# Row-tiled attention scores from the sixth pair of heads on instead of the seventh, with a new table of due dates

## The chip, the cores and the metric

The kernel runs on one core of a Trainium2 chip, as one program in which TensorE (PE), VectorE (DVE), ScalarE (ACT), GpSimd (POOL) and SyncE (SP) work side by side. The metric is the device time of one execution in microseconds. The kernel before took 307.12 us, the median of five runs (306.81 to 309.54).

## The reference

Two layers follow each other. The first is block-sparse attention over 4 batches, 8 heads, 768 tokens and 64 features a head. The mask goes by blocks of 32 tokens: neighbours, the first and last block, and three drawn blocks a query block.

```python
scores = scale * np.matmul(q, k.transpose(0, 1, 3, 2))
mask = np.abs(blk_i - blk_j) <= window
mask = mask | (blk_i == 0) | (blk_j == 0) | (blk_i == n_blocks - 1) | (blk_j == n_blocks - 1)
...                                     # and the sampled blocks of each query block
attn = softmax(np.where(mask, scores, -1e9))
return np.matmul(attn, v)
```

The heads are put side by side (768 x 512 a batch) and go through a residual MLP:

```python
a1 = alpha1 * x + beta1
u = x + lam * np.einsum('ts,bsd->btd', w_tok, a1)       # mixes tokens
a2 = alpha2 * u + beta2
return u + lam * (np.maximum(a2 @ w_ch1, 0.0) @ w_ch2)  # 512 -> 2048 -> 512
```

## The kernel before

**Pairs and units.** The 32 (batch, head) combinations are taken as 16 pairs of heads, four pairs a batch. Scores are computed transposed, keys on partitions, and each pair's 2 x 768 x 768 scores are cut into 9 units of 128 x 1024. A unit goes through four steps: its scores on TensorE into PSUM; the exponential on ScalarE into an SBUF tile `eT` (seven of them), line 1057; in the row form a multiplication with the mask on VectorE, line 1062; and the product with the values on TensorE, line 1081, which also gives the sums for the division (lines 1097 and 1100).

**Two forms of scores**, told apart by `T0`. Pairs below `T0` use the *full* form. Their q and k are transposed by TensorE (line 517, twelve transposes a pair), four copies bring them from PSUM to SBUF (lines 576 on ScalarE, 578 on VectorE), and a matmul contracts over 88 rows: 64 features and 24 rows that hold the mask as a bias (line 1019). One unit is one operation of the planner. Pairs from `T0` on use the *row-tiled* form (`prep_rows`). Their q and k are transposed by DMA on SP's queue, three transfers a pair (lines 915 and 938); the two halves of each query buffer are also needed on the other 64 partitions, which two moves do (line 959; DMAs for pairs 6 and up, VectorE copies for a pair below 6). The contraction has 64 rows, and two matmuls run at once in the upper and lower half of the array (line 1038). One operation of the planner is a batch of three units; two of the units lie in two-bank PSUM tiles (`sps`), the third in two single banks (`gb`), whose exponential is done in two halves. The mask of the row form is computed once, by 12 small matmuls from the buffers of pair `T0 - 1` (line 806), an exponential (line 820) and ten copies into `msk` (line 832 and one after it).

**The other stages.** After a batch's pairs are normalised, x is scaled and shifted (lines 1253 and 1264), tokens are mixed (`tok`, line 1302, with w_tok transposed on TensorE at the start), u is formed (lines 1326 and 1340), and the two channel matmuls follow (`ch1`, line 1449, its ReLU at line 1488 on ScalarE or 1496 on VectorE; `ch2`, line 1529, and the last sum at line 1551). The scaling vectors `lam`, `a1` (alpha1), `b1` (beta1) and `a2` (alpha2) are loaded as broadcasts; token mixing needs the first three.

**What sets the order.** A planner (`Plan`) writes the program. Each operation has a list of engines that can run it with a cost, dependencies, the buffers it needs, and a due date in units (about 1 us apart). `Plan.run` steps through modelled time and gives each idle engine, among the operations that are ready and find their buffers free, the one with the smallest due date; the instructions are emitted in that order, and the order is fixed on each engine. Loads run in one modelled queue (`queued`), SP's transfers beside them (`beside`). A pair's transposed q and k have two buffers in all (`qk`), and raw q, k and v four each. A due date is a base from a formula plus a hundredth of an entry of the table `DUE`, entry by entry in the order in which the operations were added:

```python
for op, x in zip(pl.ops, DUE):
    op.due += x * 0.01
pl.run()
```

The first entries are those of wtk 0 to 2 (bases -4, 1, 2), the broadcasts lam, a1, b1, a2 (8, 8.1, 8.2, 16), four parts of w1 (24 to 27), then k, q and v of each pair. The base of the loads of q and k is `9 * pi - 12` for pairs below `T0` and `9 * pi - 20` from it on.

Of the kernel before, what the change touches and what calls it, by code (L numbers as in the profile page):

```python
# [45 lines left out]
T0 = 6  # L46
FINE = 3
DUE = [
    -3320, -4973, -4124, -2497, -3795, -94, -4291, 3313, 2359, 2331, -861, -5555, -5734, -3452, -4351, -4448,
    -4315, -638, -1806, 2418, 1986, -1493, 1958, 1931, -1716, 1224, 1688, -2528, 53, 1439, -341, 3700, 125,  # L50
    742, -4865, 5401, 2785, 4715, -531, -4901, -2475, 3984, 913, -3830, 5751, 9883, -2111, -215, 10152, -5717,
    1842, -7686, 748, -1316, 16146, 1379, -1773, -1993, -1719, -178, -17140, 2893, -11188, -12305, -3457, 182,
    -6674, -6907, -2346, -10621, -794, 3980, -5076, -203, 2648, -1691, -2758, -3166, -3178, 11068, -2537,
    -3434, 7487, -1999, -10741, -4678, -7266, -870, -10374, -996, 0, 0, 0, 0, 0, 0, 0, 0, 0, 0, 0, 0, 0, 0, 0,
    0, 0, 0, 0, 0, 0, 0, 0, 0, -5099, -6292, -10397, -6299, 3643, -7374, -10673, -9328, -6545, -2679, 2050,
    3212, -7799, -10612, -10005, -9083, -4760, -10523, -13207, -5336, -3600, -6148, 5224, -13270, 894, -1963,
    4971, -8368, 19587, 4850, 6731, -2817, 5395, -19447, 2663, 5944, -9167, -10839, -8054, -2150, 5871,
    -11026, -3278, -5093, 5470, -1761, -735, 182, 5882, 2231, 3836, -6607, -963, -84, 3197, -5604, -4701,
    -8847, -4544, 1423, -5386, -3880, -2292, -1085, -2445, 5311, -3851, 4130, -2333, -694, 0, 0, 9060, -11409,
    -3670, -6195, 0, 0, 4307, -1082, -5729, -10780, 0, 0, 3630, -2020, -5854, -6594, -788, 992, 2804, 310,  # L60
    486, -4798, 2399, -1962, 4764, 118, 3925, 7540, -5227, -3529, 6170, -2580, 5023, 757, -3488, -5436, 1160,
    5708, 5926, 3276, -6650, 6353, 8432, 4371, 3728, 6630, -5542, -4044, 4798, 6193, -6752, 5993, 8994, -533,
    1275, -5131, -7973, -10760, 861, -8296, -12995, -6273, -1450, -8559, -6956, -6232, -677, -5807, -6900,
    -10086, 1173, -7413, -3525, 4331, 1542, -5413, -2264, -8282, -15528, -3823, -11284, -344, -6138, -10239,
    -1938, -9077, 2100, -10737, -11446, 5447, 1599, -5555, -9202, -11839, -6291, -6113, -767, -3507, -4951,
    3673, -7548, -4630, 6000, -3463, -3921, 461, 3395, -1614, 3316, -7396, 5447, -2586, 5102, 378, -540,
    -2951, 4594, 880, -406, -1267, 5243, -4379, 8689, 4355, 3064, -3464, -5400, -1231, 8372, 1238, 7813,
    -7145, 5460, -6781, -3993, -5397, 5226, 1459, 1212, -6142, 2371, 6649, -349, -2533, 220, 4405, -34, 5109,
    4523, -5837, 2213, 124, -7774, 6239, -8726, 5220, -1036, -3161, -487, -1056, -13293, 3244, -2643, 2371,
    2592, -1357, 550, 4360, -7264, 18900, -55, -2161, 5474, 3291, 6317, 3135, 3508, -15586, -7698, -6100,  # L70
    -7503, 1137, -3258, -6008, -4078, -1346, -6586, -817, -3836, 6211, 2410, 1955, -7224, -6685, -7259, 136,
    3165, -4495, -2968, 3328, -2401, 1738, -12609, -3332, -4744, -8040, 3294, -3495, -779, -4106, 3848, 173,
    -4068, 449, 3057, 1513, 5312, 2185, 2201, -2589, -1691, -2575, 5539, 1031, 10211, -2421, -923, 614, 3643,
    -704, -2117, -826, -2410, -2501, -497, -957, 4071, 683, 966, 1081, -26, -2558, 2545, -5958, -5659, -5275,
    -3076, -3121, -2934, -8288, 596, -265, 8788, -2681, 32, 3687, -3940, 4036, -345, -12468, -5978, -4694,
    -4109, -7828, -3022, -12204, -9197, -1796, -13036, 1017, -8655, -2715, 215, -12248, -1218, 7488, -4328,
    -155, 20, 312, -1077, -4136, 11082, -6529, -5888, -5300, 2783, 9055, -3505, 1177, 5249, 7142, 705, -3825,
    720, -1106, -3238, 992, -5532, 2237, -4603, 1964, -1970, 1009, -11287, -1932, -5980, -2093, -4879, -6892,
    -7820, 4360, -1100, -2993, 1852, -2438, 2137, -981, -7198, -6575, 1694, 1702, 3767, -6928, -7962, 3583,
    -9, -313, 512, 6802, 1457, 7109, -1617, 1680, -3802, -11748, 6822, 9939, -3661, -668, 4217, -365, -4539,  # L80
    -6964, 3855, 8630, -6438, 6555, -5493, 397, 1871, 104, -3907, -3520, -12610, 3890, -2298, -8952, -7709,
    -1034, 696, 3003, -5565, -11962, -6900, -7633, -2777, -2200, -3843, 5861, -5613, -591, -14430, -6326,
    1159, -282, -2272, -10693, -9822, 4015, 7719, -4088, 2380, -11269, -4553, 6242, -286, -4895, 3165, 1836,
    3998, -6333, -4739, 8162, 11837, -4302, 4438, 1835, -4226, -4645, -8200, -1834, 2630, -4607, 2490, -4646,
    9296, 3217, 3014, 8088, -1828, 1218, 4557, 1285, 1332, 557, -1916, 6043, -12, 13666, 4828, -4915, -1346,
    -537, -211, -1810, -3117, 1718, -5470, -6241, -15807, -4699, -3758, 1735, 1320, 44, -3218, -1665, -674,
    -3409, -10059, 10265, 1161, 1003, 2339, -6710, 11942, 5208, -3774, -3373, -287, 4786, 4702, -5032, -661,
    874, 4162, -2466, 1539, -8357, -4375, -6611, -13472, -6697, -1302, 6112, 2597, -5260, -3454, -719, -7674,
    -4425, 1397, -201, 4462, -7237, -4471, 4190, 13085, 7488, 12366, 11408, 6073, -6413, -4366, -5909, -736,
    -801, -5381, 8333, 3871, 1899, -9586, -7333, -1970, 4774, -20, 1963, 5481, 1546, 7302, 3234, 4459, -3025,  # L90
    2524, 116, -5796, 2307, 3971, -857, 1183, 1185, -2394, -526, 9256, -4431, 2692, 8027, -6981, 9387, 979,
    -2400, 6532, 463, -1237, 3375, -2440, -3084, -11031, -3313, -8817, 3237, -12826, -412, 10805, 3442,
    -23829, -5087, 7711, 4847, 5045, -2820, 10599, 4625, 6705, 20731, 4944, 14197, 4144, 8980, 10175, -1121,
    6493, -342, 8838, 4280, 11178, 12600, 71, 6755, 13382, 584, -8512, -7532, -9377, 5505, 4922, 1188, 12796,
    12696, 12651, 21122, -2065, -3302, -4344, 424, -2662, -9160, -7126, -3927, -2624, -8204, -2640, 5219,
    -6189, 1350, -8839, -1613, -307, -3382, -703, 4460, -3373, -6771, -2302, -415, -3014, 5547, 5378, 2103,
    -149, 3588, 9640, 9236, 10329, 3977, 989, -63, 3536, -3956, -793, 823, 6219, -10205, 5510, -5653, -2158,
    -2265, -4052, 2538, -3992, -2730, -5898, 1903, -240, -5846, -5735, -5358, -2361, 1826, 1234, -246, 967,
    -141, -6788, 2256, 3669, -332, -5309, -4898, -6464, -523, 125, 2070, 993, -4256, -8406, 23, -7868, -2579,
    -1517, -3907, -2545, -7444, 4499, 2201, 2305, -4315, -716, -847, 1109, -837, -1865, 823, 620, -74, 3256,  # L100
    62, 618, -3542, -824, 6019, -1828, 1584, 4025, -2170, 4111, -4414, -3854, -4591, -1217, -4567, -2014, 100,
    3587, -2582, 1206, -6364, 636, 1239, 8009, -1897, 1751, 6060, 1080, -9779, 4499, -1225, -7744, -4604,
    -1748, -4068, -11085, -4489, -7447, -1652, 1972, 2416, -7520, -3783, 4563, -731, 573, -163, 1736, -6327,
    2720, 4442, -2964, -2233, -6335, -4681, 447, -3120, 4487, -4525, 1368, -6234, 4316, 571, -655, 5271, 3958,
    -5701, -5374, -5929, -5950, 2436, -5387, -665, -2333, 9969, -12579, -703, 201, 3405, 813, 5509, -863, 375,
    3698, -5396, -8886, 4957, 4553, 358, -3480, -6286, 5126, -119, 4979, 537, -9373, -4074, -3406, -1563,
    4030, 7977, 5202, -10863, 2264, -5107, 4188, -4549, 3252, -6595, -36, -2835, 2186, -3110, -1052, 3721,
    -9708, -6967, -5167, -7406, -11272, 7752, 876, -8691, 619, -7394, -5574, -1069, 3293, -2643, 2523, -7011,
    -975, 5444, -5258, 1155, -2123, -3704, -1937, -2176, -11087, -3670, 2625, 7632, -9034, 58, -510, 2162,
    -2293, -3097, 5274, -3580, -4226, 3684, 9443, -1440, -884, -5931, -4516, -5482, -8502, -2036, -4404,  # L110
# [254 lines left out]
def kernel(  # L365
# [274 lines left out]
    def load_pair(pi, what="qkv"):  # L640
        b, n = divmod(pi, NPAIR)
        for w in what:
# [3 lines left out]
            def emit(op, key=key, src=src, w=w):  # L646
# [4 lines left out]
                1000,  # L651
                9 * pi - (6 if w == "v" else 12 if pi < T0 else 20),
                emit,
# [143 lines left out]
    def mask_ops():  # L797
        key = ("mmr",)
        due = 9 * T0 - 10

# [263 lines left out]
    def emit_pv(op, part, pi, u, a):  # L1064
# [3 lines left out]
        for c in part:  # L1068
# [3 lines left out]
            r = s % 36  # L1072
            if pi < T0:
                jt, t = divmod(r, NT)
# [543 lines left out]
```

## Time and profile before

| | before |
|---|---|
| median of five runs | 307.12 us |
| profiled execution | 307.31 us, span 305.5 us |
| granted clock of TensorE | 1.00 |
| instructions | 7143 |
| busy PE / DVE / ACT / POOL | 297.0 / 234.1 / 177.3 / 44.6 us |
| DMA | 31.38 MB, mean 103 GB/s; over 160 GB/s in nearly all of the first 75 us |

The span runs from the first to the last instruction of the profiled execution. Busy time of PE overstates its work, since a matmul is recorded from its start to its modelled end and the next one starts before that; start-to-start distances in the timeline are the better measure. In the lists of instruction groups, a line gives the source line, engine, operation, tiles, shape and count, then busy time and mean length, then the engine's idle time before them and who ended it.

Landings of the first loads by the trace's semaphore events, in us from the span's start (the order is that of issue):

| k1 | q1 | wtk1 | wtk2 | k2 | q2 | wtk0 | v1 | v2 | a1 | a2 | lam | k3 | b1 | q3 |
|---|---|---|---|---|---|---|---|---|---|---|---|---|---|---|
| 9.32 | 10.48 | 12.28 | 14.13 | 16.47 | 16.83 | 18.61 | 19.65 | 20.61 | 22.07 | 24.10 | 25.20 | 26.19 | 26.82 | 28.09 |

The next ones are k6 28.79, k4 29.75, v8 30.76 and w1 (its last quarter) 33.24. The last part of w1 lands at 48.76, the last of w2 at 63.30.

### The profile page before, as it was taken

How to read it: one execution, taken by the hardware profiler on the slowest of the kernel's cores; microseconds unless marked ns; L12 is line 12 of the kernel's file. 1: busy time of each engine (PE TensorE's matmuls, PEld its weight loads, DVE VectorE, ACT ScalarE, POOL GpSimd, SP SyncE). 2: the span in 40 equal slices, each digit the busy share in tenths (PEclk: the TensorE clock that was granted, in tenths of full speed). 3: DMA queues.
4: the chain of work that ended last, by engine and by line, in shares of the span. 5: the costliest groups of instructions: out<-in, count | busy, mean ns of one | idle time of the engine just before them, and what ended most of it. 6: DMA issues, size and time to landing. Idle time of an engine off the chain costs nothing.

```text
span 305.5 us, 7143 instructions
## 1 busy us (share of the span) xinstructions
PE 297.0 (97%) x2970; PEld 186.4 (61%) x2991; DVE 234.1 (77%) x441; ACT 177.3 (58%) x242; POOL 44.6 (15%) x71
## 2 busy tenths in 40 slices
PE   7897999999999999999999999999999999999996
PEld 3675888766666576466655565555664674565443
DVE  7777889988988995979877896668868682897212
ACT  5897998987788755775477655654657720000000
POOL 9456533140210110020000000000000000000000
PEclk9999999999999999999999999999999999999999
DMA  7999999999895879074171544050020004000111
GB/s 163 190 198 208 204 204 185 179 209 168 123 158 98 138 133 163 7 130 103 28 126 34 115 54 79 35 137 11 36 52 36 34 2 121 36 0 0 71 65 72
DMA packets 50672, 31.38 MB, mean 103 GB/s; under 512 B 27784, under 2 KB 47056, under 8 KB 50640
## 3 DMA queue, kind: packets, MB, share of 16 engines
q0 software_dynamic: 17520, 15.47, 33.4%
q1 hardware_dynamic: 32796, 15.06, 22.8%
q8 instruction: 23, 0.38, 0.5%
q10 hardware_dynamic: 324, 0.39, 0.4%
q14 instruction: 9, 0.07, 0.1%
HBM read 30.78 MB, written 6.29 MB: 121 GB/s over the span
## 4 chain that ended last, share of the span: by engine, by line
PE 88%; DMA 7%; POOL 2%; issue 1%; ACT 1%; DVE 0%; POOLq 0%; ACTq 0%
PE gb L1449 27%; PE gb L1529 27%; PE gb L1302 10%; PE gb L1081 10%; PE sps L1019 5%; PE sps L1038 4%; DMA wtk<-in_moe_w_tok_dram 4%; PE gb L1038 3%; DMA q<-in_q_dram 3%; PE gb L517 1%; POOL k L647 0%; ACT eT L1057 0%; POOL q L647 0%; ACT qk L576 0%; POOL wtokT L469 0%
## 5 line engine op out<-in xcount | busy, mean ns | idle before, releaser
L1057 ACT ACTIVATE eT<-sps 128x1024 f16<-128x1024 f32 x114 | 110.6, 1029 | 11.0 <-PE gb L1081 5.7
L1449 PE MATMUL gb<-uT,w1b 128*128 128x384 bf16 (+1 forms) x512 | 91.8, 326 | 0.0
L1529 PE MATMUL gb<-w2b,hts 128*128 128x512 bf16 (+2 forms) x379 | 87.2, 370 | 1.1
L1449 PEld LDWEIGHTS <-w1b 128*128 128x128 bf16 x512 | 48.5, 98 | 33.7 <-issue 1.9
L1062 DVE TENSOR_TENSOR eT<-eT,msk 128x1024 f16<-128x1024 f16 x90 | 59.6, 683 | 6.4 <-ACT eT L1057 6.4
L1529 PEld LDWEIGHTS <-hts 128*128 128x128 bf16 x400 | 36.6, 98 | 38.9 <-issue 1.9
L1057 ACT ACTIVATE eT<-gb 128x512 f16<-128x512 f32 x60 | 32.5, 594 | 33.8 <-PE gb L1038 31.8
L1496 DVE TENSOR_SCALAR hts<-gb,b1t 128x384 bf16<-128x384 f32 x73 | 44.8, 616 | 9.1 <-PE gb L1449 7.6
L1081 PEld LDWEIGHTS <-eT 128*128 128x128 f16 x1152 | 44.3, 97 | 10.8 <-issue 2.2
L1081 PE MATMUL gb<-vext,eT 128*128 128x65 f16 x1152 | 47.9, 193 | 0.1
L1488 ACT ACTIVATE hts<-gb,b1t 128x384 bf16<-128x384 f32 x55 | 31.5, 582 | 21.3 <-PE gb L1449 19.1
L1302 PE MATMUL gb<-a1p,wtokT 128*128 128x256 bf16 (+1 forms) x360 | 37.0, 251 | 0.0
L1551 DVE TENSOR_TENSOR ot<-x_sb,gb 128x512 f32<-128x512 f32 (+2 forms) x25 | 16.6, 664 | 26.0 <-PE gb L1529 26.0
L1302 PEld LDWEIGHTS <-wtokT 128*128 128x128 bf16 x360 | 29.5, 98 | 6.9 <-issue 1.9
L1019 PE MATMUL sps<-qk 88*128 88x512 bf16 (+1 forms) x144 | 31.3, 325 | 0.6 <-ACT eT L1057 0.3
L1326 DVE TENSOR_TENSOR x_sb<-x_sb,gb 128x512 f32<-128x512 f32 (+1 forms) x26 | 16.7, 641 | 2.8 <-PE gb L1302 2.4
L1100 DVE TENSOR_TENSOR x_sb<-gb,rcp 128x384 f32<-128x384 f32 x32 | 17.8, 557 | 1.1
L1038 PE MATMUL sps<-qk 64*128 64x256 bf16 x180 | 17.9, 305 | 0.0
L1340 DVE TENSOR_TENSOR ub<-x_sb,a_bc 128x512 bf16<-128x512 f32 (+1 forms) x26 | 16.1, 644 | 0.3
L1097 DVE RECIPROCAL rcp<-gb 128x6 f32<-128x6 f32 x32 | 6.1, 192 | 13.3 <-PE gb L1081 13.2
L1038 PEld LDWEIGHTS <-qk 64*128 64x128 bf16 x240 | 9.3, 94 | 11.5 <-issue 7.1
L647 POOL DMA_DIRECT2D v<-in_v_dram x15 | 10.6, 704 | 36.3 <-DVE vext L1119 24.7
(70 smaller groups left out, 171.1 us busy)
## 6 DMA issues: line engine op xcount, KB each, us to landing
out_dram<-ot SPq DMA_DIRECT2D x23, 256.0 KB, 2.1
v<-in_v_dram POOLq DMA_DIRECT2D x16, 192.0 KB, 8.5
k<-in_k_dram POOLq DMA_DIRECT2D x15, 192.0 KB, 7.6
q<-in_q_dram POOLq DMA_DIRECT2D x15, 192.0 KB, 7.6
w1b<-in_moe_w_ch_dram POOLq DMA_DIRECT2D x4, 512.0 KB, 11.3
w2b<-in_moe_w_ch_dram POOLq DMA_DIRECT2D x4, 512.0 KB, 17.4
qk<-qk SPq DMA_DIRECT2D x20, 96.0 KB, 2.5
wtk<-in_moe_w_tok_dram POOLq DMA_DIRECT2D x3, 384.0 KB, 8.4
```

Source lines behind the costliest of these rows:

```text
L1019: nc.tensor.matmul(spsT[sl(key[0])][:, o : o + w], kx2[i][0:KC, a, ts(jt, P)], qx2[i][0:KC, a, c : c + w], start=True, stop=True,)
L1038: nc.tensor.matmul(half(key, r)[:, o : o + w], kd[i][rows, h, g, :], qx2[i][rows, h, c : c + w], start=True, stop=True,)
L1057: nc.scalar.activation(out_, in_, AF.Exp, bias=EXPB, scale=SCALE)
L1062: nc.vector.tensor_tensor(out=e, in0=e, in1=msk[:, :, x : x + 512], op=ALU.mult)
L1081: nc.tensor.matmul(bk[:, t * VW : t * VW + D + 1], eTt[sl(("eT", i))][:, ts(col, P)], vx[:, a, jt, 0 : D + 1], start=(r == 0), stop=(r >= ...
L1100: nc.vector.tensor_tensor(out=x_sb[:, s0 : s0 + NT, h * D : (h + 1) * D], in0=o[:, :, 0:D], in1=rc[:].unsqueeze(2).broadcast_to([P, NT, D] ...
L1302: nc.tensor.matmul(bank(bk)[:, j * wp * P : (j + 1) * wp * P], wtokT[:, s, ts(m * g + j, P)], a1p[sl(ak)][:, s, 0:wp, :].rearrange("p w c ...
L1326: nc.vector.tensor_tensor(out=s, in0=s, in1=tp, op=ALU.add)
L1449: nc.tensor.matmul(bank(bk)[:, 0 : HS + w0], w1b[:, dk, ts(f, P)], rhs[dk], start=(dk == 0), stop=(dk == 3),)
L1488: nc.scalar.activation(htsT[hk][:, f, :], bank(bk)[:, w0 : HS + w0], AF.Relu, bias=b1t[:, f : f + 1], scale=1.0,)
L1496: nc.vector.tensor_scalar(out=htsT[hk][:, f, :], in0=bank(bk)[:, w0 : HS + w0], scalar1=b1t[:, f : f + 1], scalar2=0.0, op0=ALU.add, op1=A ...
L1529: nc.tensor.matmul(bank(ck)[:, cs], htsT[hk][:, nk, ts(mt, P)], w2h["t"][:, nk, cs], start=(nk == 0), stop=(nk == 15),)
```

## The change

`T0` goes from 6 to 5, and every entry of `DUE` is replaced. The planner, its costs and its modelled landing times, the operations and the buffers stay as they are.

```diff
-T0 = 6
+T0 = 5
 FINE = 3
 DUE = [
-    -3320, -4973, -4124, -2497, -3795, -94, -4291, 3313, 2359, 2331, -861, -5555, -5734, -3452, -4351, -4448,
...
+    -3684, 199, -845, -288, -1686, -4441, 2523, 2253, 3785, 2762, -783, -617, -789, 450, 524, 817, 1058, 468,
...
 ]
```

For pair 5, `T0 = 5` takes away four TensorE operations of three transposes each, four PSUM copies and nine one-unit score operations. In their place come two DMA transposes of q and one of k, two half-swaps on VectorE (pair 5 is below 6), nine mask multiplications and three batches of row-tiled scores. Both tables have 1408 entries. The mask is built from pair 4's buffers instead of pair 5's, its base due dates are 9 earlier, and the loads of q and k of pair 5 have the base 25 instead of 33.

## The prediction

> **What bounds the kernel now.** I read the busy shares, then the chain that ended last, then TensorE's own waits. The two lines below, from the page, give busy time and the chain by engine.
>
> ```profile
> PE 297.0 (97%) x2970; PEld 186.4 (61%) x2991; DVE 234.1 (77%) x441; ACT 177.3 (58%) x242; POOL 44.6 (15%) x71
> ...
> PE 88%; DMA 7%; POOL 2%; issue 1%; ACT 1%; DVE 0%; POOLq 0%; ACTq 0%
> ```
>
> Busy PE alone would prove little, since a matmul's recorded length overlaps the next one's. The chain says more: 88% of the span is TensorE after TensorE, and the 7% of DMA lies before 28.1 us. The waits of PE say the same, in us, times, longest:
>
> ```profile
> PE gb L517 <- DMA q<-in_q_dram: 1.7, 1, 1.7
> PE gb L517 <- DVE relp L512: 1.0, 1, 1.0
> PE gb L485 <- PEq L1602: 0.8, 1, 0.8
> PE gb L517 <- ACT relp L541: 0.4, 1, 0.4
> PE gb L485 <- DVE ot L1551: 0.4, 1, 0.4
> PE sps L1019 <- ACT eT L1057: 0.3, 1, 0.3
> ```
>
> All of PE's waits make 4.6 us, and after 30 us there is no single one above 0.3 us but a dummy matmul at the very end. The granted clock is 1.00 in every stretch that the windows below show. So a microsecond of TensorE work that goes away is a microsecond off the end, as long as no other engine or transfer makes PE wait in its place.
>
> **PE work removed and added.** From the timeline of PE I take distances from start to start. The first lines hold pair 5 (the sixth) as it is now, the last ones a batch of three row-tiled units of a later pair (columns: start, length, instruction, count).
>
> ```profile
> 57.17 1.04 PE L1019 MATMUL sps<-qk 88*128 88x512 bf16 x5
> 58.05 0.33 PE L517 MATMUL gb<-identb,q 128*128 128x128 bf16 x3
> 58.22 0.33 PE L517 MATMUL gb<-identb,k 128*128 128x128 bf16 x3
> 58.38 0.82 PE L1449 MATMUL gb<-uT,w1b 128*128 128x385 bf16 x4
> 59.04 0.60 PE L1019 MATMUL sps<-qk 88*128 88x256 bf16 x3
> 59.48 2.13 PE L1449 MATMUL gb<-uT,w1b 128*128 128x385 bf16 x12
> ...
> 87.08 0.54 PE L1081 MATMUL gb<-vext,eT 128*128 128x65 f16 x12
> 87.55 0.39 PE L1038 MATMUL gb<-qk 64*128 64x512 bf16 x2
> 87.78 0.60 PE L1038 MATMUL sps<-qk 64*128 64x256 bf16 x6
> 88.31 0.82 PE L1449 MATMUL gb<-uT,w1b 128*128 128x384 bf16 x4
> ```
>
> Two full units (five matmuls) take 58.05 - 57.17 = 0.88, one takes 59.48 - 59.04 = 0.44 us: nine units 3.94. Three transposes take 0.17 (58.05 to 58.22); pair 5 has twelve: 0.67. Both go. A row-tiled batch takes 88.31 - 87.55 = 0.76 us from its first matmul to the next other one. Before it, 12 matmuls of 65 columns, at 65/128 of a transpose's 0.056 us so 0.028 to 0.03 each, end near 87.46, so entering costs about another 0.09. Three batches: 3 x 0.85 = 2.55. Saved: 3.94 + 0.67 - 2.55 = **2.06 us**. The 12 small matmuls for the mask (L806) only move from pair 5 to pair 4.
>
> *The skill on this.* The Trainium skill, "TensorEngine Tiling (Array Packing)", section Theoretical Speedup, gives up to 2x for a contraction of 64 or less; its section Key Properties says that a change of tiling mode drains the array. By 2x alone the three batches would cost 1.97 and the saving be 2.64; the trace's 2.55, with the 0.09 us at the entry of a batch, is the drain at work, and the trace decides.
>
> **VectorE and ScalarE.** The row form masks after the exponential instead of in the matmul. From the page's groups:
>
> ```profile
> L1057 ACT ACTIVATE eT<-sps 128x1024 f16<-128x1024 f32 x114 | 110.6, 1029 | 11.0 <-PE gb L1081 5.7
> L1062 DVE TENSOR_TENSOR eT<-eT,msk 128x1024 f16<-128x1024 f16 x90 | 59.6, 683 | 6.4 <-ACT eT L1057 6.4
> L1057 ACT ACTIVATE eT<-gb 128x512 f16<-128x512 f32 x60 | 32.5, 594 | 33.8 <-PE gb L1038 31.8
> ```
>
> DVE gains nine mask multiplications, 9 x 0.683 = 6.15. It gains two half-swaps (for this pair on DVE, not by DMA), which the trace lacks: bounded by 0 and by the dearest copy of 768 columns within SBUF, 0.456 (L996); I take the nearest in width and speed, 0.351 (L1119), so 0.7 and at most 0.9. Of the four PSUM copies of pair 5 that go, one ran on DVE (0.56) and three on ACT (3 x 0.789 = 2.37). In each batch one exponential of 1029 ns becomes two of 594: ACT gains 3 x 0.159 = 0.48. Net: DVE +6.3, ACT -1.9 us. The ten mask copies (L832: 9 of 404 to 594 ns, about 4 us in all with the last) move up from 72 to 76 us, ahead of pair 5's first multiplication.
>
> Do these find room? Columns of the windows: stretch, length, busy us of PE, PEld, DVE, ACT, POOL, clock, DMA share, GB/s.
>
> ```profile
> 28.00:57.00 29.00, 28.83 (x474) 24.13 (x474) 26.07 (x53) 26.37 (x29) 12.37 (x18) 1.00 1.27 199
> 57.00:73.00 16.00, 15.90 (x170) 10.64 (x170) 13.68 (x37) 12.82 (x19) 4.91 (x7) 1.00 1.30 194
> 73.00:110.00 37.00, 36.84 (x369) 22.44 (x370) 34.47 (x66) 29.14 (x43) 6.33 (x9) 1.00 0.81 124
> ```
>
> Pair 5's scores lie in 57 to 73. DVE and ACT idle there for 2.3 + 3.2 = 5.5 us; wanted are 6.3 - 1.9 + 4 = 8.4. The excess of 2.9 us must go to neighbours, and ACT alone idles 7.9 us in 73 to 110. ReLUs can run on either engine (616 ns on DVE, 582 on ACT), so about ten of them moving to ACT rebalance it. I cost this at nothing; if the cover fails, 2.9 us shared by two engines hold PE up by about 1.5.
>
> *A rule that speaks against the change.* The same page, section PSUM Bottleneck, warns that tiling speeds up TensorE but not the emptying of PSUM. By the trace that is so: pair 5's exponentials go from 9.26 to 9.74 us while its scores go from 3.94 to 2.55. Were ACT the bound in this stretch, the change would cost 0.5 us instead of gaining 2. PE's waits on ACT after 30 us are 0.3 at most, so I go by PE.
>
> **Transfers.** Three DMA transposes are added on SP, about 1.23 + 1.23 + 1.28 us to issue. SP's queue is empty from 2.8 to 45.3 us; behind them stand only pair 6's transposes. When they land matters more. For the keys (L938, first four issues) the trace says
>
> ```profile
> DMA to landing us min/median/max: 3.1/8.3/13.4
> ```
>
> and the 13.4 belongs to the only one issued in the full stretch before 60 us (issued 47.96; the first of its queries at 45.26). If pair 5's follow the same course, issue to landing takes 61.4 - 45.3 = 16.1 us in all. They need the score buffer that pair 2 or pair 3 leaves: scores of 27 units end near 34 us, of 36 near 44, so they land near 50 or near 60, and are wanted near 55 to 57. By the new table the loads of pair 5's keys and queries rank 17th and 19th (due 33 and 37, from a base of 9 x 5 - 20 = 25), five loads behind pair 3's queries, which land near 27.6 (below); at one a microsecond both are there by about 32.6, before pair 2's buffer is free; SP is idle and takes it at once, as it did for pair 6 at 45.26. So I take the early landing and cost it at nothing. What the transposes take from the loads is bounded by 0 and by their issue time, 3.7 us; the last w1 lands 48.8 and the first use is 56.1, the last w2 63.3 against 73.6, which covers it.
>
> **The new table.** It moves every instruction. Order of the loads by due date (base + table/100) so far: k1, q1, wtk1, wtk2, k2, q2, wtk0, v1, v2, a1, a2, lam, k3, b1, q3. Now: wtk0, b1, k1, q1, a1, wtk2, wtk1, lam, v1, q2, k2, k3, w1, q3. With the trace's distances between landings (v2 0.96, a2 2.03 gone from ahead of q3, one w1 2.48 put there) q3 lands at 28.09 + 2.48 - 2.99 = 27.6, hardly sooner. But lam and b1 land near 19 instead of 25.2 and 26.8, so token mixing (first at 30.8 us now, after b1) could fill the 1.7 us that PE waits for q3. Against it, q2 and k2 land near 22 instead of 16.8, and pair 2's exponentials start at about 24.7: with 1.6 for transposes and copies that just fits. The gain is bounded by 1.7, the loss by a similar size; I take zero, since what is gained at 28 may be lost at 23.
>
> **Sum.** The profiled execution takes 307.31 (span 305.5), the median of the runs is 307.12. 307.31 - 2.06 = 305.25; from the median 305.06. I say **305.2**. One per cent, 3.1 us, is about what a measurement of this kernel can tell from no change.
>
> **Rivals.**
> - *Early wait goes too* (chance 0.25): 305.2 - 1.7 = 303.5. For it: lam and b1 six microseconds earlier. Against: k2, q2 and v2 are later.
> - *DVE and ACT become the bound* (0.20): the squeeze of 57 to 73 comes back as PE waits of 1.5 to 3 us, and the time is 306.5 to 308. For it: DVE over 90% busy from 40 to 60 us. Against: ACT's idle time later.
> - *Pair 5's transposes come late* (0.15), the side that is slower: if they get pair 3's buffer (44 us) they land near 60 and, at 45.3 as pair 6 did, at 61.4. PE takes its instructions in order, so a batch put at 56 stands 4 to 5.4 us, and with it all later work: 305.2 + 4 to 5.4 = 309 to 310.6. It decides from a landing past 58 on, where the wait exceeds the 2.06 gained.
>
> The forecast has 0.40. Below 304.05 lie most of the first rival and little else: 0.26. Above 310.2 lie the worst of the last rival and a table worse in places I can't see: 0.14. The range takes in the first rival with a little more, and most of the last: 302.6 to 309.8.
>
> **What would show it.** Right: 120 matmuls at L1019 instead of 144, 198 at L1038 instead of 180, 48 transposes of q and k instead of 60, 99 multiplications at L1062 instead of 90, PE without waits over 0.5 us from 50 to 75. Wrong: PE waiting for qk's landing or for eT near 55, ACT idle after L1038 at 57, or a new wait on k2 or v2 at 22 to 29. I'm wrong if PE's sum of waits changes by over 2 us.

## The result and the profile after

The changed kernel takes 306.31 us (median of 45 runs) against 307.37 for the kernel before (85 runs beside them). The ratio is 0.9956, with a 95% interval of 0.9945 to 0.9967: 1.35 us less, between 1.0 and 1.7. Of the 85 executions of before 22 took 308.5 us or more and none of the 45 of the changed kernel did (in the executions of before that were measured beside the experiments those of that length show a granted clock of 0.994 or less), and without them the median of before is 307.12 us and the gain 0.81. The forecast was 305.2, so the sign and the range held, and 0.8 to 1.35 of the 2.06 us came. The profiled execution took 306.62 us (span 304.8), 0.69 less than that of before. The kernel before has this one profile; after_again below is a second one of the changed kernel. Line numbers are 2 lower than before (L1017 are the full scores, L1036 the row-tiled ones).

Busy time and the chain by engine, from the page of the changed kernel:

```profile
PE 298.3 (98%) x2959; PEld 185.8 (61%) x2979; DVE 234.3 (77%) x444; ACT 179.2 (59%) x249; POOL 45.0 (15%) x71
...
PE 85%; DMA 9%; ACT 2%; DVE 1%; issue 1%; SPq 1%; ACTq 0%
```

Busy PE went up by 1.3 us although PE lost work. Part of it is the start (last section): until 9.7 us this execution's matmuls ran at half speed. The chain has a new term, which the next view names. Its groups, with count, busy time and mean:

```profile
L1055 ACT ACTIVATE eT<-sps 128x1024 f16<-128x1024 f32 x111 | 108.0, 1034 | 3.0 <-PE sps L1017 2.2
...
L1060 DVE TENSOR_TENSOR eT<-eT,msk 128x1024 f16<-128x1024 f16 x99 | 64.9, 683 | 3.8 <-ACT eT L1055 3.5
...
L1055 ACT ACTIVATE eT<-gb 128x512 f16<-128x512 f32 x66 | 35.9, 595 | 39.2 <-PE gb L1036 38.2
...
L1017 PE MATMUL sps<-qk 88*128 88x512 bf16 (+1 forms) x120 | 27.8, 338 | 0.4 <-DVE qk L576 0.2
...
L1036 PE MATMUL sps<-qk 64*128 64x256 bf16 (+1 forms) x198 | 19.9, 305 | 0.0
```

The counts are those of the forecast: 120 full matmuls, 198 row-tiled ones, 99 multiplications, 48 transposes of q and k (line 515, not shown), three exponentials fewer from `sps` and six halves more from `gb`. The waits of PE, in us, times, longest:

```profile
PE gb L483 <- PEq L1600: 0.8, 1, 0.8
PE gb L1036 <- DMA qk<-qk: 0.5, 1, 0.5
PE gb L483 <- DVE ot L1549: 0.4, 1, 0.4
PE gb L1079 <- DVE vext L1117: 0.2, 1, 0.2
PE gb L1447 <- ACT hts L1486: 0.2, 1, 0.2
PE sps L1017 <- DVE qk L576: 0.2, 1, 0.2
```

The wait of 1.7 us for pair 3's queries is gone. New is the second line: a row-tiled batch stands for a DMA that writes `qk` from `qk`, that is for one of the half-swaps. Where it stands is seen in PE's timeline (start, length, instruction, count, wait):

```profile
59.23 0.39 PE L1036 MATMUL gb<-qk 64*128 64x512 bf16 x2
59.46 0.60 PE L1036 MATMUL sps<-qk 64*128 64x256 bf16 x6
59.99 6.08 PE L1447 MATMUL gb<-uT,w1b 128*128 128x385 bf16 x36
...
75.06 0.39 PE L1036 MATMUL gb<-qk 64*128 64x512 bf16 x1
75.97 0.37 PE L1036 MATMUL gb<-qk 64*128 64x512 bf16 x1 [0.52 <-DMA qk<-qk]
75.98 0.80 PE L1036 MATMUL sps<-qk 64*128 64x256 bf16 x6
76.71 0.42 PE L1079 MATMUL gb<-vext,eT 128*128 128x65 f16 x8
```

The three batches of pair 5 (the first at 59.23) run undisturbed at the expected 0.76 us. The batch that is held up belongs to pair 6, which was row-tiled before as well: from 75.06 to 76.71 it takes 1.65 us, 0.89 more than one without a wait. DVE and ACT in the stretches of the forecast, from the windows (columns as there):

```profile
28.00:57.00 29.00, 28.84 (x465) 23.43 (x463) 27.69 (x60) 27.76 (x33) 12.64 (x17) 1.00 1.26 199
57.00:73.00 16.00, 15.78 (x157) 9.64 (x156) 15.38 (x44) 14.78 (x25) 5.02 (x8) 1.00 1.39 178
73.00:110.00 37.00, 36.32 (x382) 21.93 (x384) 33.08 (x59) 27.22 (x41) 6.99 (x10) 1.00 0.93 134
```

Both are fuller in 57 to 73 us (DVE 15.38 of 16, ACT 14.78), and PE stays at work but for 0.16 us (on a ReLU of ScalarE at 67 us). What PE loses in 73 to 110 lies at 75 us.

### The profile page after: what moved, and what is told of

It is laid out like the page before. It is cut to its first block, busy times and chain, and to the rows that moved or that the text cites. A ratio compares the mean times of both kernels' runs of the same rounds, so it can differ in the third digit from the quotient of the medians.

```text
span 304.8 us, 7139 instructions
## 1 busy us (share of the span) xinstructions
PE 298.3 (98%) x2959; PEld 185.8 (61%) x2979; DVE 234.3 (77%) x444; ACT 179.2 (59%) x249; POOL 45.0 (15%) x71
## 4 chain that ended last, share of the span: by engine, by line
PE 85%; DMA 9%; ACT 2%; DVE 1%; issue 1%; SPq 1%; ACTq 0%
PE gb L1527 26%; PE gb L1447 23%; PE gb L1079 10%; PE gb L1300 10%; DMA k<-in_k_dram 5%; PE sps L1017 4%; PE sps L1036 4%; DMA qk<-qk 3%; PE gb L1036 3%; ACT eT L1055 2%; PE gb L483 1%; PE gb L515 1%; SPq L936 0%; DVE qk L576 0%; SPq L957 0%
## 5 line engine op out<-in xcount | busy, mean ns | idle before, releaser
L1055 ACT ACTIVATE eT<-sps 128x1024 f16<-128x1024 f32 x111 | 108.0, 1034 | 3.0 <-PE sps L1017 2.2
L1447 PE MATMUL gb<-uT,w1b 128*128 128x384 bf16 (+1 forms) x508 | 89.5, 326 | 0.2 <-ACT hts L1486 0.2
L1060 DVE TENSOR_TENSOR eT<-eT,msk 128x1024 f16<-128x1024 f16 x99 | 64.9, 683 | 3.8 <-ACT eT L1055 3.5
L1055 ACT ACTIVATE eT<-gb 128x512 f16<-128x512 f32 x66 | 35.9, 595 | 39.2 <-PE gb L1036 38.2
L1079 PE MATMUL gb<-vext,eT 128*128 128x65 f16 x1152 | 49.9, 193 | 0.4 <-DVE vext L1117 0.2
L1494 DVE TENSOR_SCALAR hts<-gb,b1t 128x384 bf16<-128x384 f32 x69 | 42.3, 615 | 9.8 <-PE gb L1447 8.4
L1017 PE MATMUL sps<-qk 88*128 88x512 bf16 (+1 forms) x120 | 27.8, 338 | 0.4 <-DVE qk L576 0.2
L1036 PE MATMUL sps<-qk 64*128 64x256 bf16 (+1 forms) x198 | 19.9, 305 | 0.0
L1036 PEld LDWEIGHTS <-qk 64*128 64x128 bf16 x264 | 10.5, 94 | 13.9 <-issue 9.2
L1251 DVE TENSOR_TENSOR a1p<-x_sb,a_bc 128x768 bf16<-128x768 f32 (+1 forms) x17 | 15.4, 906 | 0.2
L1262 DVE TENSOR_TENSOR a1p<-a1p,b_bc 128x768 bf16<-128x768 bf16 (+1 forms) x17 | 15.4, 904 | 0.2
```

Of the source, the lines that this page charges most:

```text
L1017: nc.tensor.matmul(spsT[sl(key[0])][:, o : o + w], kx2[i][0:KC, a, ts(jt, P)], qx2[i][0:KC, a, c : c + w], start=True, stop=True,)
L1036: nc.tensor.matmul(half(key, r)[:, o : o + w], kd[i][rows, h, g, :], qx2[i][rows, h, c : c + w], start=True, stop=True,)
L1055: nc.scalar.activation(out_, in_, AF.Exp, bias=EXPB, scale=SCALE)
L1060: nc.vector.tensor_tensor(out=e, in0=e, in1=msk[:, :, x : x + 512], op=ALU.mult)
L1079: nc.tensor.matmul(bk[:, t * VW : t * VW + D + 1], eTt[sl(("eT", i))][:, ts(col, P)], vx[:, a, jt, 0 : D + 1], start=(r == 0), stop=(r >= ...
L1447: nc.tensor.matmul(bank(bk)[:, 0 : HS + w0], w1b[:, dk, ts(f, P)], rhs[dk], start=(dk == 0), stop=(dk == 3),)
```

## Experiments

Theory at the start: PE sets the end, a microsecond of PE work counts in full, and about 2 us of work did go; what is missing was lost at a few places that vary from run to run or that I hadn't counted. Rivals: DVE is the real bound around pair 5, or the new table is worse in places and eats the rest.

**after_again: the changed kernel once more.**

> The changed kernel as it is, for comparison on the same chip and for a second look at its start. Both theories: 0.9945 to 0.9967 of the kernel before, near 306.0 us. In its first profile TensorE ran at half speed (512 columns in 0.43 us) until 9.65 us, in that of the kernel before only until 3.5 us, though both programs are the same up to there. If that is chance and not the table, this profile may show the early switch, with a span 0.3 to 0.6 us under the first one's 304.8; if the table causes it, the switch comes at 9.6 us again.

Measured 305.94 us, ratio 0.9963 (0.9949 to 0.9977); profiled 305.62, span 303.8. In this execution pair 6's first batch has no wait, and the waits of the start are others:

```profile
PE gb L515 <- DMA q<-in_q_dram: 0.5, 1, 0.5
PE gb L515 <- DMA wtk<-in_moe_w_tok_dram: 0.5, 1, 0.5
...
PE gb L1079 <- DVE vext L1117: 0.3, 1, 0.3
```

Its last channel matmul starts at 299.45 us, against 301.41 before: PE's stream ends 1.96 us sooner. The loss at 75 us comes in some executions and not in others.

**pe_twice: does PE work count in full?** Pair 5's three batches are computed twice into the same tiles. By the trace that is 1.95 us of PE more: each takes 1.41 us instead of 0.76.

```diff
                 (emit_qk_full if pj < T0 else emit_qk_rows)(pj, uj, key)
+            if batch[0] // 9 == 5:
+                for j, key in zip(batch, keys):
+                    emit_qk_rows(5, units[j][1], key)
```

> Each of pair 5's three row-tiled batches is computed twice into the same banks: 3 x 0.66 = 1.98 us more TensorE work at the very place where the change took 2.06 away, nothing else. Theory (TensorE is the bound there, a microsecond counts in full): 2.0 us slower than the changed kernel, 1.002 of the kernel before. Rival (VectorE or ScalarE is the bound between 57 and 73 us, so the TensorE work saved there was not what counted): under 0.7 us slower.

Measured 307.50 us, ratio 1.0020 (1.0008 to 1.0032). Beside after_again that is 1.56 us by the medians and 1.75 by the ratios (0.0057 x 307); 1.95 lies within the intervals. The traces agree: from pair 5's first batch to pair 6's first PE takes 17.56 us (58.40 to 75.96) instead of 15.83 in after_again (59.13 to 74.96). PE work at this place counts in full, or nearly so.

**mask_short: is DVE the bound at pair 5?**

```diff
-        nc.vector.tensor_tensor(out=e, in0=e, in1=msk[:, :, x : x + 512], op=ALU.mult)
+        n = 32 if i // 9 == 5 else 512
+        nc.vector.tensor_tensor(
+            out=e[:, :, 0:n], in0=e[:, :, 0:n], in1=msk[:, :, x : x + n], op=ALU.mult
+        )
```

> Pair 5's nine mask multiplications are done on 2 x 32 columns instead of 2 x 512 (most of the mask is left out for this pair), which takes about 9 x 0.5 = 4.5 us from VectorE between 60 and 75 us. Theory (VectorE's extra work is covered): within 0.3 us of the changed kernel. Rival (VectorE and ScalarE are the bound there): 1 to 2 us faster.

Measured 305.90 us, ratio 0.9961 (0.9936 to 0.9987), the same as with the multiplications. DVE's added work is covered, as the forecast took it.

**k9_later: why does pair 6's half-swap come late?** By the new table the load of pair 9's keys (due 81 - 20 - 20.85 = 40.15) goes ahead of that of pair 6's keys (54 - 20 + 13.65 = 47.65; a pair's entries stand in the order q, k, v). One entry is changed, which puts it behind.

```diff
 DUE = [
...
-    -2085, -1281, 715, ...          # first entry: load of the keys of pair 9
+    0, -1281, 715, ...
```

> One entry of the new table: the due date of the load of pair 9's keys goes from 40 to 61, behind that of pair 6's keys (48). Now the keys of pair 9 take the raw buffer first, pair 6's keys land at 63.4 us, their transposes and the two swaps follow, and TensorE waits 0.9 us at 75 us for pair 6's swap. Theory (this wait is where a good part of the missing 0.7 us went): pair 6's keys land near 51, the wait goes, 0.5 to 0.9 us faster than the changed kernel, 0.993 of the kernel before. Rival (the wait only hides another one, or the swap lands late because the transfers are full): within 0.2 us of the changed kernel.

Measured 305.64 us, ratio 0.9949 (0.9925 to 0.9973): the best of all, but not to be told from after_again. The traces say more than the time. SP's queue in the changed kernel:

```profile
51.77 5.95 SPq L913 DMA_TRANSPOSE qk<-q  x2
63.42 1.21 SPq L936 DMA_TRANSPOSE qk<-k  x1
64.73 1.35 SPq L957 DMA_DIRECT2D qk<-qk  x2
```

and SP's wait between the first two lines:

```profile
SPq L936 <- DMA k<-in_k_dram: 5.6, 1, 5.6
```

The load of pair 6's keys, issued at 47.55, lands at 63.40, and the transpose goes out at 63.42, just ahead of the swaps. With the edit the load is issued at 34.46 and lands at 51.52, and SP's queue is

```profile
59.04 1.58 SPq L941 DMA_TRANSPOSE qk<-k  x1
65.53 1.36 SPq L962 DMA_DIRECT2D qk<-qk  x2
```

The transpose leaves 4.4 us sooner. The swaps do not: they wait 4.9 us more for the transposed queries. So the part of my theory by which they'd be issued sooner fell. But they land sooner after their issue, as the view of the swaps' line shows, first for the changed kernel, then with the edit:

```profile
DMA to landing us min/median/max: 2.2/4.5/10.4
```

```profile
DMA to landing us min/median/max: 2.2/4.4/6.0
```

The maximum is the second swap of pair 6. In the changed kernel it lands at 75.93, and the batch goes on at 75.97; in after_again at 74.44, half a microsecond before the batch wants it; with the edit at 72.27, for a batch at 76.43. In before the keys of pair 6 were in at 28.79, the slowest swap took 6.9 us, to about 63.4, and the batch came at 72.84. So the table turned 9 us of slack into none to half a microsecond in these two, and into 2 us at most where it stands unchanged and PE has no more work (1.6 in mask_short, 1.95 in after_lane). The profiled execution itself (307.10 us) spoils the comparison of times: it started at half speed to 9.27 us and has a wait of 0.8 us for `ub` at 35 us.

**before_late_start and after_late_start: does the slow start count?** The changed kernel's two profiles differ in the moment at which TensorE becomes fast (9.7 and 5.2 us). Four dummy matmuls of 512 columns are put into the start of each kernel.

```diff
     keep_warm(3, P)
+    keep_warm(4, 512)
     for t in vext:
```

> Four dummy matmuls of 512 columns (0.85 us at full speed, 1.7 at half) ahead of the first score matmul of the kernel before, near 5.5 us; nothing else. Theory (in the kernel before a late start is absorbed by the wait for pair 3's queries at 26 to 28 us, whose landing TensorE doesn't move): 0 to 0.3 us slower than the kernel before. Rival (TensorE is the bound from the start): 0.85 us slower or more.

> The same four dummy matmuls in the changed kernel, whose wait at 28 us is gone. Theory (nothing absorbs a late start any more): 0.85 us slower than the changed kernel or somewhat more, so a ratio to the kernel before near 0.999. Rival (both absorb it): under 0.3 us slower, 0.997. Rival (both pay): as the theory says here, but the kernel before then pays the same.

Before: 307.11 us, ratio 0.9995 (0.9982 to 1.0007). After: 306.56, ratio 0.9970 (0.9952 to 0.9988), so 0.25 us above the changed kernel by the medians and 0.4 by the ratios, where I had expected 0.85. By the times the rival is nearer. The traces settle it for the kernel before only. These are the same scores in before and before_late_start, then another set in the changed kernel and after_late_start:

```profile
28.60 0.60 PE L1019 MATMUL sps<-qk 88*128 88x512 bf16 x3
28.39 0.60 PE L1020 MATMUL sps<-qk 88*128 88x512 bf16 x3
```

```profile
21.83 0.60 PE L1017 MATMUL sps<-qk 88*128 88x512 bf16 x3
22.84 0.60 PE L1018 MATMUL sps<-qk 88*128 88x512 bf16 x3
```

In before_late_start the wait of 1.7 us for pair 3's queries is gone, PE having come later, and by 28 us nothing is left of the delay. In after_late_start PE is 1.0 us late at 22 us and still 0.8 at pair 5's first batch (60.02 against 59.23): that execution did not absorb the dummies. It took 307.13 us, 0.57 above its kernel's median, so what the delay costs the changed kernel on average stays open. Its swap lands at 76.32 for a batch that began at 75.85 and takes 1.25 us, 0.49 too many.

**after_bc_later and after_bc_again: the order of the early loads.** The loads of alpha1 and beta1 move from their places (fifth and second) to just ahead of lambda, which VectorE needs with them anyway.

```diff
     LD = {}
+    LATE = []
...
         def emit(op):
-            nc.gpsimd.dma_start(t[:], src.unsqueeze(0).to_broadcast([P, DM]))
+            if nm in ("a1", "b1"):
+                LATE.append((t, src))
+                return
+            for u, v in (LATE if nm == "lam" else []) + [(t, src)]:
+                nc.gpsimd.dma_start(u[:], v.unsqueeze(0).to_broadcast([P, DM]))
```

> In the changed kernel the loads of b1 and a1 are issued just ahead of lam instead of second and fifth; the order of everything else stays. Pair 1's keys and queries land 0.9 us sooner and the last parts of w_tok 0.7 to 1.5 us sooner; b1 and a1 land near 18.5 and 19, before lam as now. In the second profile of the changed kernel TensorE waited 0.7 us for pair 1's queries at 13 us and 0.6 us for w_tok at 16.9. Theory (these waits are what the new order of loads gives back): they go, and the time falls by 0.5 to 1.2 us to 0.993 of the kernel before. Rival (ScalarE's exponentials set the pace there, so TensorE only waits elsewhere): within 0.2 us of the changed kernel.

Measured 307.29 us, ratio 0.9992 (0.9970 to 1.0014): 1 us slower than the changed kernel, not faster. The profile fell on an execution of 1156 us (last section), so a second measurement follows.

> The same kernel as after_bc_later (the loads of alpha1 and beta1 issued just ahead of lambda's), whose median was 1 us above the changed kernel's and whose profile showed nothing useful, because TensorE ran at a quarter of its speed in it. Question: is the order of loads the cause? Theory A (the order costs): this profile has, in 10 to 35 us, a new wait of TensorE or later token mixing that makes about 1 us against the changed kernel's second profile, in which TensorE waits 0.5 us for q, 0.5 us for w_tok and 0.3 us for the values' copy at 13 to 22 us; time about 307.2, ratio to the kernel before 0.999 or more. Theory B (the order costs nothing; both vectors wait for lambda on VectorE anyway, and w_tok lands up to 1 us sooner, so that the 0.5 us at 17 us is gone): the profile has no new wait over 0.3 us, PE's last channel matmul starts at 299.0 to 300.5 us, and the time is 305.5 to 306.4, ratio 0.994 to 0.998; the 1 us of the first measurement was then not the order's.

Measured 307.80 us, ratio 1.0010 (0.9988 to 1.0032), so the order does cost. Two of PE's waits and the two lines of VectorE's timeline behind the first one:

```profile
PE gb L1084 <- DVE vext L1122: 1.8, 1, 1.8
PE gb L1041 <- DMA qk<-qk: 1.4, 1, 1.4
```

```profile
20.62 0.43 DVE L768 CAST lam_bcb<-lam_bc 128x512 bf16<-128x512 f32 x1 [1.80 <-DMA lam_bc<-in_moe_lam_dram]
...
22.03 0.35 DVE L1122 COPY vext<-v 128x768 f16<-128x768 f16 x1
```

Lambda has the same place in the order but lands at 20.59 instead of 19.47, and VectorE stands 1.80 us for it, with the copy of pair 1's values behind in its order; PE, a microsecond ahead by then, waits 1.84 us for that copy. What PE had gained at 13 to 20 us is spent, and more: its losses in 10 to 30 us are 0.5 us above after_again's. Everything then comes later: pair 6's swaps are issued at 66.10, land at 77.66, and hold the batch of 75.92 up by 1.76 us. So the larger part of this kernel's loss is again the swap. Through a link without slack an early delay is handed on, here enlarged: half a microsecond at 30 us, 1.76 at 76.

**after_lane: the end of the program.** From the end of the last transfer to the end of the span the changed kernel takes 1.61 us, before 1.33. SP closes the program with waits on the semaphores of its transfers in a fixed order, 0.06 us apart. The last output sits on a semaphore with one such wait behind it before, and with six behind it in the changed kernel, which issues three more transfers on SP. Six early outputs are issued as two halves, which moves the last output's place.

```diff
-                def e_out(op, okey=okey, b=b, t=t, cs=cs):
-                    nc.sync.dma_start(
-                        out[b].rearrange("(p o) d -> p o d", o=NT)[:, t, cs],
-                        ot[sl(okey)][:, cs],
-                    )
+                def e_out(op, okey=okey, b=b, t=t, cs=cs, kk=kk):
+                    for c in [slice(0, HS), slice(HS, DM)] if kk < 2 else [cs]:
+                        nc.sync.dma_start(
+                            out[b].rearrange("(p o) d -> p o d", o=NT)[:, t, c],
+                            ot[sl(okey)][:, c],
+                        )
```

> At the end SP waits for the semaphores of all its transfers in one fixed order, about 0.06 us a wait. In the kernel before the last output's semaphore is the second last of that order, in the changed kernel (three transfers more on SP) the third: five waits more stand behind its landing, and the span ends 0.28 us later after the last transfer. Here six early output transfers are issued as two halves each, so that the last output gets the last semaphore of the order. Theory: from the end of the last transfer to the end of the span 1.25 to 1.3 us instead of 1.61, 0.3 us faster than the changed kernel, 0.995 of the kernel before. Rival (the end is set by something else, such as the engines' last handshakes): the same end, same time.

The end took 1.27 us, as expected; the time was 306.50, ratio 0.9983 (0.9962 to 1.0005), no gain, where 0.995 was expected. In its place stands a new wait:

```profile
PE gb L1036 <- issue: 1.5, 1, 1.5
```

"issue" means that the view found no releaser. It is a swap again, of a later pair: the batch starts at 137.97, and the swap that was issued last lands at 137.88. SP spends 0.98 us on the two halves of an output ahead of these swaps, where one piece takes 0.34, and its transposes before them are about a microsecond later too, so the swaps are issued from 132.28 on instead of 131.06; in after_again the later of them lands at 136.10 for a batch at 136.32.

**t5_old_table and t6_new_table: the table and T0 apart.** The old offsets, carried over by the operations' names, with `T0 = 5`; the new ones with `T0 = 6`. An operation that exists in one kernel only takes the offset of its counterpart in the neighbouring pair. The second kernel is the changed one with

```diff
-T0 = 5
+T0 = 6
```

> The row form from pair 5 on, with the old table carried over operation by operation (the new operations of pair 5 get the offsets of pair 6's and pair 6's multiplications). Theory (TensorE's work is 2.06 us less in any order, but a table fits its own operations alone): slower than the kernel before by 2 to 3%, 313 to 317 us, with waits of TensorE spread from 10 to 80 us. Rival (the 2.06 us are what counts and the table adds little): 305 to 307.

> The other half: the full form for pair 5, with the new table carried over (its transposes and copies get pair 4's offsets). Theory: slower than the kernel before by 2 to 3%, 313 to 318 us. Rival (the new table is what made the kernel faster): 306 to 308.

With the old table the change of `T0` gives 319.80 us, ratio 1.0414 (1.0375 to 1.0453); the new table without it gives 311.01, ratio 1.0125 (1.0095 to 1.0154). Both are slower, as expected, but both lie outside what I had expected, the first above 317 and the second below 313. About 3.4 us of the first are not the order's alone: its trace has two stretches of 3.4 us at half clock (last section; the mean clock of its four executions is 0.976 to 0.989). That is an estimate from their lengths, and by it the time would lie near 316 without them. PE's largest waits with the old table:

```profile
PE gb L522 <- DVE x_sb L1331: 2.6, 1, 2.6
PE gb L1043 <- DVE hts L1501: 1.8, 2, 1.5
PE gb L1086 <- DVE eT L1067: 1.7, 2, 1.0
PE gb L1454 <- ACT hts L1493: 1.5, 3, 0.9
```

With the offsets carried over in this one way, a table fits the operations it was found for; other ways weren't tried. The 2 us of work come out only with an order in which PE has no such waits; DVE and ACT, covered in the changed kernel, are not covered here. The two parts of the change can't be priced as a sum.

**before_a2_late: can the kernel before have the early wait's 1.7 us?** The load of alpha2, needed last, moves behind that of pair 3's queries.

```diff
     LD = {}
+    LATE = []
...
+                if key == ("q", 3):
+                    LATE.pop()()
...
-            nc.gpsimd.dma_start(t[:], src.unsqueeze(0).to_broadcast([P, DM]))
+            go = lambda: nc.gpsimd.dma_start(t[:], src.unsqueeze(0).to_broadcast([P, DM]))
+            if nm == "a2":
+                LATE.append(go)
+            else:
+                go()
```

> In the kernel before, with its order of instructions, the load of a2 is issued behind that of pair 3's queries instead of ahead of lam: lam, k3, b1 and q3 land about 2 us sooner (q3 near 26.1), a2 near 28, ahead of its first use at 33.8. Theory (the wait for q3 is slack ahead of a TensorE-bound stretch, so what goes there counts in full): the wait of 1.7 us goes, 1.0 to 1.7 us faster than the kernel before, 0.995 to 0.997. Rival (a wait of the same size comes right behind, for the vectors of token mixing or ScalarE's exponentials): within 0.3 us of the kernel before.

Measured 306.07 us, ratio 0.9965 (0.9949 to 0.9981). PE's waits in it are all these:

```profile
PE gb L485 <- PEq L1609: 0.8, 1, 0.8
PE gb L485 <- DVE ot L1558: 0.4, 1, 0.4
```

A load moved by a few places in the kernel before gains as much as the whole change, within the errors (0.9965 and 0.9956), with no other instruction touched.

## Why the prediction was right, and where its sum was off

**PE is the bound, and its work counts in full: right.** pe_twice shows it at pair 5 itself.

**Saved PE work, 2.06 us: right to 0.05.** From start to start after_again's matmuls of 512, 256 and 128 columns take 0.216, 0.109 and 0.056 us. Pair 5's full form has twelve of each, 4.57 us. A row-tiled batch takes 0.756 us in the traces of before and after_again, and the matmul ahead of it 0.096 more than elsewhere, whether it has 65, 256, 384 or 512 columns: three batches are 2.56, and the saving is 2.02. (By its own 0.028 to 0.03 us a matmul of 65 columns the prediction should have had 0.11 to 0.13 at the entry; its 0.09 was the better number.) That this gap is a drain of the array, as the prediction has it, no run shows; they show the gap.

**DVE and ACT covered: right.** Full counts and fuller windows with a single PE wait of 0.16 us between 57 and 73 us, and mask_short gains nothing. ReLUs moved as foreseen, though fewer than ten: DVE has 69 on record instead of 73, ACT 58 instead of 55 (one of the 128 is missing from the trace). The half-swaps of pair 5 on DVE, which I put at 0.351 us, take 0.356 each where undisturbed.

**Pair 5's transposes: right.** Its keys and queries landed at 30.34 and 32.29 us (32.6 was the estimate), the first transpose was issued at 32.35, the last one landed at 48.74 (near 50), and the first batch came at 59.23. The rival of the late transposes fell with that.

**The early table as zero-sum: right.** q3 landed at 27.60 (27.6 foreseen), lambda at 19.21, q2 and k2 at 21.15 and 22.11. PE's losses before 57 us (time from its first matmul less each matmul at its full-speed distance from start to start) are 7.4 us in before, 7.3 in the changed kernel, 7.2 in after_again: the 1.7 us at 26 to 28 are gone and came back at 13 to 22 and at the start. Three more profiles with the same instructions up to 57 us (pe_twice, after_lane, mask_short) lose 6.5, 7.3 and 7.5, so the zero is known to about half a microsecond. The sum of PE's waits alone fell from 4.6 to 2.3 us in the changed kernel (3.1 in after_again). By the prediction's own last sign, a change by over 2 us, that would count against it; but the sum leaves out the half-speed start and the many gaps too short for the list. The first rival was right about the wait and wrong about the time. before_a2_late shows that it needn't have been so.

**The step that failed** is the sum's last: "307.31 - 2.06", with nothing else in it. Two terms are missing. One is the program's end, +0.28 us: from the last landing to the end it takes 1.27 to 1.29 us in every profile of the changed kernel and its variants but after_lane, and 0.96 to 0.99 in before and its variants. The other is pair 6's half-swap. The step on transfers asked only whether pair 5's transposes come in time and whether the weights are still covered; it didn't follow the three added transfers to what stands behind them on SP, though it named pair 6's, nor the loads of pair 6 in the new table, whose keys fell from 28.79 to 63.40 us. Its own sign of failure, "PE waiting for qk's landing", came, but at 75 us and from pair 6. With these terms the sums nearly close: 307.31 - 2.02 + 0.28 = 305.57 without the swap's wait (after_again's profile: 305.62) and 0.89 more with it, 306.46 (the changed kernel's: 306.62). The median of 306.31 lies between, as it would if some executions have the wait and some not. The profiles of the same table show both: 0.89 and 0.49 us in the changed kernel and after_late_start, none at this place in after_again, pe_twice, mask_short and after_lane. What decides it is open. TensorE's late start may have a part in it: in both profiles with the wait TensorE becomes fast late (9.7 and 9.9 us), in three without it early (4.6 to 5.2), but in after_lane late too (9.7). That k9_later's edit acts on the cause is shown by the second swap's landing, 6.0 us after its issue, against 8.7 to 10.5 in these six profiles; that it makes the kernel faster is not shown, since the times with and without the edit can't be told apart.

## What to carry to other kernels

When a step is added to a queue, follow it to the next transfer behind it, and ask of each link how much slack it had and has; the cost was at pair 6, not at pair 5, where I looked. A fitted table of due dates belongs to its operations: price the whole, never the parts, and compare when each load is issued, not only those of the pair that changes. Before new arithmetic is tried, look for a wait that a load in the wrong place makes: here it was worth as much.

## What the runs showed of the hardware

**TensorE starts at half speed, and when it becomes fast differs from execution to execution.** The same five matmuls, with the dummies after them, in the timeline of before and then of the changed kernel:

```profile
5.54 1.03 PE L1019 MATMUL sps<-qk 88*128 88x512 bf16 x5
6.41 0.57 PE L485 MATMUL gb<-const-bfloat16-1.0 128*128 128x128 bf16 x7
```

```profile
5.91 1.87 PE L1017 MATMUL sps<-qk 88*128 88x512 bf16 x5
7.57 0.95 PE L483 MATMUL gb<-const-bfloat16-1.0 128*128 128x128 bf16 x7
```

From start to start they take 0.87 and 1.66 us. The switch came at 3.5 us in before, at 9.7 and 5.2 in two profiles of the same changed kernel, and between 4.2 and 10.0 in the others. The windows show a granted clock of 1.00 all the while: the trace's first record of the clock begins only at the switch (3.6 us in before, 9.7 in the changed kernel). The Trainium skill, "TensorE: Matmul & The Clock Gate", Part 1, describes a gate that opens after a busy window of about 3.4 us that runs free of the kernel's start, and gives half speed as 107 ns for 128 columns; the 0.107 us measured here agrees, a switch as late as 10 us is later than one such window. Between the changed kernel's two profiles the difference is gone by 22 us, where the scores shown at before_late_start begin at 21.83 us with the late switch and at 22.00 with the early one, since PE waits for loads in between.

**TensorE can fall back to half speed in the middle of a kernel.** Two windows of t5_old_table, and the stretch between them (columns as before; the clock is the third number from the end):

```profile
49.90:53.30 3.40, 3.31 (x22) 2.22 (x20) 3.06 (x7) 3.15 (x4) 0.53 (x2) 0.51 1.13 155
53.30:87.50 34.20, 29.13 (x344) 18.76 (x342) 28.98 (x72) 23.95 (x36) 8.75 (x13) 1.00 1.15 160
87.50:90.90 3.40, 3.12 (x13) 1.12 (x14) 0.23 (x1) 2.70 (x5) 0.00 (x0) 0.50 0.58 83
```

In both, 512 columns take 0.43 us instead of 0.216. The first comes 0.9 us after a wait of PE of 2.55 us, the second after waits of 0.6, 1.0 and 0.3 us within 3 us. The waits of 1.8 us in after_bc_again and 1.5 us in after_lane are followed by none, so what sets it off is not settled here. By estimate a stretch of 3.4 us at half speed costs up to 1.7 us on top of the wait.

**A quarter of the speed, and less.** In one execution of after_bc_later 512 columns took 1.28 us until about 230 us and 0.84 us from then on, instead of 0.216, and the whole 1156 us. The windows show a granted clock of 1.00 there too, but the trace holds no record of the clock. What caused it is open, and it was seen once.

**A transfer's landing depends on what is ahead of it.** The same 64-partition swap lands 2.2 us after its issue at best and 10.8 at worst (in after_bc_again), the worst ones right behind a key transpose while the loads still fill the DMA engines.
